# Output matmuls of chosen stretches as four column tiles of TensorE, with a new planner cost for instruction fetch and a new list of departures

## The chip, the cores and the metric

The kernel runs on one core of a Trainium2 chip. The time is the device time of one execution in microseconds (us), as the median of its runs. PE is TensorE, ACT ScalarE, DVE VectorE, POOL GpSimd and SP the engine that issues most DMAs here.

## The reference

An attention over 32 inducing points comes first, then a two-way maxout layer; the output of the first is the input of the second.

```python
def mab(q, kv):                      # scale = 1/sqrt(128)
    s = scale * (q @ kv.transpose(0, 2, 1))
    s = s - s.max(-1, keepdims=True)
    a = np.exp(s)
    a /= a.sum(-1, keepdims=True) + 1e-09
    return a @ kv
h = mab(I, x)                        # I: (4, 32, 128), x: (4, 12544, 128)
y = mab(x, h).reshape(50176, 128)
out = np.maximum(y @ w1, y @ w2) @ w_out     # w1, w2: (128, 1024), w_out: (1024, 128)
```

## The kernel before

The four batches of `x` have 98 chunks of 128 tokens each. Pooling (`mab(I, x)`) of batch 0 is done in the opening, about the first 23 us. Pooling of batches 1 to 3 is interleaved with the second part of the batch before: `pool_scores` (L329, scores of 16 chunks on column tiles), an exponential on ACT, a transpose by DMA (`pool_turn`) and `pool_accum` (L385, the weighted sum, on column tiles). The small matmuls of `small_rep` to `small_m1` then give the pooled `h` of a batch and, from it, `hwd` = h times (w2 - w1) and `m1` = h times (w1 w_out).

The second part works on the identity max(a, b) = a + relu(b - a). With the attention weights e of a chunk (32 inducing points by 128 tokens), a + relu(b - a), times `w_out`, is e times `m1` plus relu(e times `hwd`) times `w_out`. Four quarters of the array's rows work on four chunks side by side:

- `stage` (L610) computes scores of up to 16 chunks on four column tiles, ACT takes the exponential into `e2`.
- `phase` issues one row wave (L1069): four row tiles of 32 rows, each into a PSUM bank of its own. A tile is either a unit of b - a ("U", `hwd` by `e2`, 512 columns in all) or the linear part of a group ("L", `e2` by `m1`). A unit's bank is read by ACT (L1085) or DVE (L1088), which writes relu to SBUF and frees the bank.
- `final_one` issues one output matmul (L876): 128 relu features of one chunk against 128 rows of `w_out`, on the full array, added to the group's bank. Eight of them per chunk, 3136 in all.
- `dens` (L671) sums the attention weights for the denominators; `evict_group` (L907) multiplies by the reciprocal on DVE, and the stores go out from the SP queue.

PE changes its tiling between row waves (`row`), column-tiled jobs (`col`) and everything else (`full`).

The order of all engines' instructions is written out while the program is built. A planner, the class `Clock`, keeps a time for PE, ACT, DVE and the eight PSUM banks; it adds a constant for each step (`PAIR`, 0.0558 us, for an output matmul; `SWITCH` for a change of tiling). The loop at L1248 asks at each step whether a wave's banks are free by that time, whether the next output matmul's relu is ready, and whether a column job is due (`column_work`: a `stage`, a `pool_scores` or a `pool_accum`; jobs fall due by the number of finished chunks), and issues the one or the other. `DEV` is a list of departures: by the step's number it says that a wave is held back (1), put forward (2), that no column job may come (3) or that one may come sooner (4).

```python
            early = 0.2 if ck.mode == "col" else 0.0
            now = tp <= ck.pe + early or tp <= tf and tf > ck.pe
            if how == 1 and tf < INF:
                now = False
            if how == 2 and tp <= ck.pe + 0.2:
                now = True
```

Every program on PE is a stream of pairs, one weight load and one matmul. A column-tiled matmul (`tile_position` (0, 32 p)) uses 32 columns of the array and writes 32 partitions of PSUM; four with different p stand side by side.

Of the kernel before, what the change touches and what calls it, by code (L numbers as in the profile page):

```python
# [19 lines left out]
class Clock:  # L20
# [3 lines left out]
    SWITCH = {"full": 0.11, "row": 0.097, "col": 0.097}  # L24
    LAT = 0.20
    SEM = 0.05

    def __init__(self):
        self.pe = self.act = self.dve = 0.0
        self.mode = "full"  # L30
        self.bank = [0.0] * 8
        self.idle = {}
        self.log = []
        self.busy = {}

# [6 lines left out]
    def run(self, us, mode="full", ready=0.0, why="data"):  # L42
        if mode != self.mode:
            self.pe += self.SWITCH[mode]
            self.busy["sw"] = self.busy.get("sw", 0) + self.SWITCH[mode]
            self.mode = mode
        self.wait(ready, why)
        self.pe += us
        self.busy[mode] = self.busy.get(mode, 0) + us
        return self.pe + self.LAT  # L50

# [51 lines left out]
def kernel(  # L103
# [9 lines left out]
    nc = tc.nc  # L113
# [82 lines left out]

    with tc.manual_schedule(engines={ET.PE, ET.DVE, ET.Activation, ET.Pool, ET.SP}):
# [32 lines left out]
        def p1_transpose(i, piece):  # L230
            k0, n = parts[0][i]
            g, m = COPY[i][piece][:2]
            bi, ps = bank([128, 8, 128], F16)
            for j in range(m):
                nc.tensor.transpose(ps[:, j, :], xn_at[0, i][:, g + j, :], identity16)  # L235
# [17 lines left out]
        def p1_scores(i):  # L253
# [3 lines left out]
            for j in range(n):  # L257
                nc.tensor.matmul(  # L258
                    out=ps[:, j * M : (j + 1) * M],
                    lhsT=xT_tiles[0][:, k0 + j, :],  # L260
                    rhs=inducingT,
                    start=True,
                    stop=True,
                )
# [15 lines left out]
        def p1_esum(i):  # L280
# [4 lines left out]
            for m in pieces(n):  # L285
                nc.tensor.matmul(
# [11 lines left out]
        def p1_hsum(i, lo=0, hi=P1):  # L298
# [3 lines left out]
            for j in range(lo, min(hi, n)):  # L302
                nc.tensor.matmul(  # L303
# [19 lines left out]
        def pool_scores(b, u):  # L323
# [4 lines left out]
            for g in range(4):  # L328
                nc.tensor.matmul(  # L329
# [16 lines left out]
        def pool_rest(b):  # L346
# [3 lines left out]
            for j in range(REST):  # L350
                nc.tensor.matmul(
# [17 lines left out]
        def pool_accum(b, u):  # L369
# [10 lines left out]
            for v in (u - 1, u):  # L380
                eT = st[b]["eT", v][0]
                st[b]["sum", v] = True
                for j in range(4):
                    for g in range(4):
                        nc.tensor.matmul(  # L385
# [8 lines left out]
            if last:  # L394
                et = st[b]["et"][0]
                for g in range(4):
# [6 lines left out]
                    for lhsT, rhs, lo, n in pairs:  # L403
                        nc.tensor.matmul(
# [21 lines left out]
        def small_rep(b):  # L426
# [3 lines left out]
            nc.tensor.matmul(out=ps[:, 0 : C + 1], lhsT=repd, rhs=st[b]["hacc"], start=True, stop=True)  # L430
# [8 lines left out]
        def small_h(b):  # L439
# [3 lines left out]
            nc.tensor.transpose(ps[:, 0:128], st[b]["h4"], identity16)  # L443
# [23 lines left out]
        def small_hwd0(n, eng=0):  # L467
# [8 lines left out]
            nc.tensor.matmul(out=ps, lhsT=st[0]["hT4"], rhs=w21[:, sl], start=True, stop=True)  # L476
# [9 lines left out]
        def small_sums():  # L486
# [3 lines left out]
            nc.tensor.matmul(out=ps[:, 2:3], lhsT=rep32, rhs=es, start=True, stop=True, skip_group_check=True)  # L490
# [7 lines left out]
        def small_hwd(b):  # L498
            st[b]["hwd"] = smp.tile([128, J], F16, name=f"hwd_{b}", tag="hwd")
            hwd = st[b]["hwd"]  # L500
            for half in range(2):
# [3 lines left out]
                nc.tensor.matmul(out=ps, lhsT=st[b]["hT4"], rhs=w21[:, sl], start=True, stop=True)  # L505
# [9 lines left out]
        def small_m1(b):  # L515
            bi, ps = bank([128, 512])
            ck.wait(max(ck.bank[bi], st[b]["hT4r"]), "p1")
            nc.tensor.matmul(out=ps[:, 0:128], lhsT=st[b]["hT4"], rhs=w1out, start=True, stop=True)
# [22 lines left out]
        def weights_2(g, eng):  # L541
            bi, ps = bank([128, 4, 128], F16)
            ck.wait(ck.bank[bi], "w")
            for j in range(4):
                jb = 4 * g + j
                nc.tensor.transpose(ps[:, j, :], w1h[:, 128 * jb : 128 * (jb + 1)], identity16)
# [8 lines left out]
        def weights_3():  # L555
            bi, ps = bank([128, 512])
            ck.wait(max(ck.bank[bi], w_of["w1T"]), "w")
            for jb in range(NJB):
                nc.tensor.matmul(
# [36 lines left out]
        def stage(blk, now=True):  # L596
# [4 lines left out]
            for q in range(4):  # L601
# [7 lines left out]
                for t, c, n in pieces:  # L609
                    nc.tensor.matmul(  # L610
# [45 lines left out]
        def dens(blk):  # L656
# [11 lines left out]
            for blk in blks:  # L668
                wd = blk.width
                for t in range(wd):  # L670
                    nc.tensor.matmul(  # L671
# [8 lines left out]
            end = ck.run(0.029 * n)  # L680
# [30 lines left out]
        def fill(n):  # L711
            bi, ps = bank([128, 512])
            for _ in range(n):
                nc.tensor.matmul(out=ps, lhsT=warm[:, 0:128], rhs=warm, start=True, stop=True)
            ck.run(0.22 * n)
# [5 lines left out]
        for _ in range(WARM):  # L721
            nc.tensor.matmul(out=ps, lhsT=warm[:, 0:128], rhs=warm, start=True, stop=True)
# [29 lines left out]
        def p1_inducing():  # L752
            bi, ps = bank([128, 512])
            nc.tensor.transpose(ps[:, 0:M], ind_sb, identity32[0:M, 0:M])
# [37 lines left out]
        state = {"g": 0, "mm": 0, "lin": 0, "done": 0, "issued": 0}  # L792
# [28 lines left out]
        def keep_busy(until):  # L821
# [6 lines left out]
            turn = ck.SWITCH["full"] if ck.mode != "full" else 0.0  # L828
# [3 lines left out]
            for _ in range(n):  # L832
                nc.tensor.matmul(  # L833
# [5 lines left out]
                    skip_group_check=True,  # L839
                )  # L840
            ck.run(0.11 * n)
# [3 lines left out]
        def linear_last(end):  # L845

            while held:
                g = held[0]
                if g.full:
                    if st[g.blk.b].get("m1r", INF) > ck.pe:  # L850
                        return
                    for s, (q, t) in enumerate(g.chunks):
                        nc.tensor.matmul(  # L853
# [5 lines left out]
                            skip_group_check=True,  # L859
                        )  # L860
                    end = ck.run(0.056 * len(g.chunks))
                evict_group(held.pop(0), end)

        def final_one():
# [4 lines left out]
            if g.ps is None:  # L869
# [6 lines left out]
            nc.tensor.matmul(  # L876
# [5 lines left out]
                skip_group_check=True,  # L882
            )
            end = ck.run(ck.PAIR)
# [75 lines left out]
        def want_linear():  # L960
# [32 lines left out]
        }  # L993
        LIMIT = -16
# [16 lines left out]
        def phase(jobs):  # L1011
# [13 lines left out]
            if ck.mode != "row":  # L1025
                ck.pe += ck.SWITCH["row"]
                ck.mode = "row"
# [38 lines left out]
            for i in range(4):  # L1066
                for seq in parts_:
                    if i < len(seq):
                        nc.tensor.matmul(**seq[i])  # L1069
# [177 lines left out]
        step = -1  # L1247
        while state["g"] < len(groups) or held:  # L1248
            step += 1
            how = DEV.get(step, 0)  # L1250
            side_work()
            if held and ck.mode == "full":
# [14 lines left out]
            early = 0.2 if ck.mode == "col" else 0.0  # L1267
# [52 lines left out]
```

## Time and profile before

| | |
|---|---|
| median of 3 runs | 325.12 us (324.23 to 325.51) |
| span of the profiled execution | 322.5 us (its page gives no time beside the span) |
| PE busy | 315.6 us, 5375 matmuls and as many weight loads |
| ACT busy, DVE busy | 281.8 us, 281.4 us |
| output matmuls (L876) | 3136, 216.9 us |
| row waves (L1069) | 888 matmuls by `hwd`, 381 by `e2` |

The span runs from the first to the last instruction of the profiled execution; the time of a run also holds what lies before and after it. Matmuls are pipelined, so a matmul's duration is longer than its distance to the next one. In the views of groups and of instructions in order of time, "L876" is line 876 of the kernel before, names are out<-in, and the idle time of an engine stands behind a bar or in brackets with what ended it.

### The profile page before, as it was taken

How to read it: one execution, taken by the hardware profiler on the slowest of the kernel's cores; microseconds unless marked ns; L12 is line 12 of the kernel's file. 1: busy time of each engine (PE TensorE's matmuls, PEld its weight loads, DVE VectorE, ACT ScalarE, POOL GpSimd, SP SyncE). 2: the span in 40 equal slices, each digit the busy share in tenths (PEclk: the TensorE clock that was granted, in tenths of full speed). 3: DMA queues.
4: the chain of work that ended last, by engine and by line, in shares of the span. 5: the costliest groups of instructions: out<-in, count | busy, mean ns of one | idle time of the engine just before them, and what ended most of it. 6: DMA issues, size and time to landing. Idle time of an engine off the chain costs nothing.

```text
span 322.5 us, 12605 instructions
## 1 busy us (share of the span) xinstructions
PE 315.6 (98%) x5375; PEld 239.8 (74%) x5375; DVE 281.4 (87%) x508; ACT 281.8 (87%) x561; POOL 37.8 (12%) x90
## 2 busy tenths in 40 slices
PE   7899999999999999999999999999999999999996
PEld 3776777777777777777777777777777777777786
DVE  3369999988989998999989989988998999899974
ACT  3779999998978999999898999998869999999960
POOL 7470000000040000000040000000006400302000
PEclk9999999999999999999999999999999999999999
DMA  8999999954279999794279999893424322324233
GB/s 205 207 268 213 218 249 203 210 136 133 100 150 245 221 254 216 181 194 139 99 151 242 218 258 207 160 211 120 118 96 103 135 80 100 109 100 128 87 118 116
DMA packets 77320, 53.99 MB, mean 167 GB/s; under 512 B 56112, under 2 KB 64976, under 8 KB 77264
## 3 DMA queue, kind: packets, MB, share of 16 engines
q1 hardware_dynamic: 71232, 39.42, 50.0%
q0 software_dynamic: 5888, 13.70, 21.7%
q8 instruction: 42, 0.69, 0.9%
q14 instruction: 14, 0.11, 0.1%
q10 hardware_dynamic: 144, 0.07, 0.1%
HBM read 27.28 MB, written 25.69 MB: 164 GB/s over the span
## 4 chain that ended last, share of the span: by engine, by line
PE 93%; DMA 5%; ACT 1%; issue 1%; POOL 0%; DVE 0%; POOLq 0%
PE ps L876 62%; PE ps L1069 22%; DMA xn<-in_x_dram 5%; PE ps L610 2%; PE ps L385 2%; PE ps L329 1%; PE ps L671 1%; PE ps L833 1%; ACT e L629 0%; PE ps L505 0%; ACT hwd L482 0%; PE ps L235 0%; PE ps L303 0%; PE ps L430 0%; PE ps L258 0%
## 5 line engine op out<-in xcount | busy, mean ns | idle before, releaser
L1085 ACT ACTIVATE relu<-ps 128x512 f16<-128x512 f32 x462 | 244.1, 604 | 23.0 <-PE ps L1069 15.0
L1088 DVE TENSOR_SCALAR relu<-ps 128x512 f16<-128x512 f32 x322 | 206.1, 682 | 16.2 <-PE ps L1069 14.8
L876 PE MATMUL ps<-woutp,relu 128*128 128x128 f16 x3136 | 216.9, 220 | 0.0
L876 PEld LDWEIGHTS <-relu 128*128 128x128 f16 x3136 | 176.6, 98 | 39.4 <-issue 28.9
L1069 PE MATMUL ps<-e,hwd 32*128 32x512 f16 (+2 forms) x888 | 88.2, 358 | 0.1
L907 DVE TENSOR_TENSOR o<-ps,rp 128x512 f32<-128x512 f32 (+3 forms) x80 | 51.2, 640 | 1.8 <-PE ps L876 1.3
L1069 PEld LDWEIGHTS <-hwd 32*128 32x128 f16 x888 | 24.5, 91 | 20.9 <-issue 0.8
L1069 PE MATMUL ps<-m,e 32*128 32x128 f16 x381 | 38.7, 217 | 0.0
L1069 PEld LDWEIGHTS <-e 32*128 32x128 f16 x381 | 21.2, 92 | 2.9 <-issue 0.4
L907 DVE TENSOR_TENSOR o<-ps,rpt 128x512 f32<-128x512 f32 (+3 forms) x28 | 17.3, 618 | 4.1 <-PE ps L853 2.2
L166 POOL DMA_DIRECT2D xn<-in_x_dram x33 | 17.8, 553 | 6.7 <-DMA xn<-in_x_dram 4.6
L164 POOL COPY pace<-hacc 128x1 f32<-128x1 f32 x2 | 0.4, 188 | 133.1 <-DVE hacc L418 133.1
L246 DVE COPY xT<-ps 128x768 f16<-128x768 f16 (+6 forms) x11 | 4.8, 458 | 8.9 <-PE ps L235 8.9
L340 ACT ACTIVATE eu<-ps 128x512 f16<-128x512 f32 x18 | 10.9, 614 | 0.1
L629 ACT ACTIVATE e<-ps 128x512 f16<-128x512 f32 (+2 forms) x21 | 10.4, 568 | 0.2 <-PE ps L610 0.2
L235 PE MATMUL ps<-identity,xn 128*128 128x128 f16 x98 | 8.1, 219 | 2.3 <-DMA xn<-in_x_dram 1.8
L535 POOL COPY m1bd<-m 32x128 f16<-32x128 f16 x4 | 1.1, 287 | 76.7 <-DVE m L530 76.6
L249 ACT COPY xT<-ps 128x768 f16<-128x768 f16 (+5 forms) x10 | 6.5, 671 | 3.0 <-PE ps L235 2.9
L698 POOL TENSOR_TENSOR w1T<-den 128x256 f32<-128x256 f16 (+1 forms) x7 | 4.4, 633 | 38.6 <-DMA den<-e 38.6
L700 POOL TENSOR_TENSOR w1T<-w1T 128x64 f32<-128x64 f32 (+4 forms) x28 | 8.4, 302 | 2.2
L235 PEld LDWEIGHTS <-xn 128*128 128x128 f16 x98 | 5.6, 97 | 4.0 <-DMA xn<-in_x_dram 2.2
L610 PE MATMUL ps<-xT,hT 128*32 128x512 f16 (+3 forms) x114 | 8.2, 361 | 0.0
(93 smaller groups left out, 117.0 us busy)
## 6 DMA issues: line engine op xcount, KB each, us to landing
out_dram<-o SPq DMA_DIRECT2D x68, 256.0 KB, 2.8
xn<-in_x_dram POOLq DMA_DIRECT2D x24, 448.0 KB, 10.1
out_dram<-o SPq DMA_DIRECT2D x54, 128.0 KB, 1.8
wf<-in_moe_w_dram POOLq DMA_DIRECT2D x4, 256.0 KB, 5.9
xn<-in_x_dram POOLq DMA_DIRECT2D x3, 224.0 KB, 8.8
xT<-xn SPq DMA_TRANSPOSE x42, 3.8
xf<-in_x_dram SPq DMA_DIRECT2D x1, 512.0 KB, 3.7
xf<-in_x_dram SPq DMA_DIRECT2D x1, 384.0 KB, 4.2
```

Of the source, the lines that this page charges most:

```text
L166: nc.gpsimd.dma_start(out=xn_at[b, i][lo:hi, 0:n, :], in_=xr[b, lo:hi, k0 : k0 + n, :])
L235: nc.tensor.transpose(ps[:, j, :], xn_at[0, i][:, g + j, :], identity16)
L249: nc.scalar.copy(out=dst, in_=ps[:, 0:m, :])
L340: nc.scalar.activation(out=eu, in_=ps, func=AF.Exp, scale=scale, accum_out=st[b]["es"][:, u : u + 1])
L610: nc.tensor.matmul(out=ps[32 * q : 32 * (q + 1), 128 * t : 128 * (t + n)], lhsT=hq, rhs=xT[:, c : c + n, :], start=True, stop=True, tile_p ...
L629: nc.scalar.activation(out=blk.e2[:, lo:hi], in_=ps[:, lo:hi], func=AF.Exp, scale=st[0]["rs"] if blk.b == 0 else scale,)
L700: nc.gpsimd.tensor_add(acc[:, :, 0:n], acc[:, :, 0:n], acc[:, :, n : 2 * n])
L876: nc.tensor.matmul(out=g.ps[:, 128 * c : 128 * (c + 1)], lhsT=g.blk.relu[q][:, 128 * (jb * w4 + t) : 128 * (jb * w4 + t + 1)], rhs=woutp[: ...
L907: nc.vector.tensor_mul(osb[:, 0:n, :], g.ps[:, 0 : n * C].rearrange("p (s c) -> p s c", s=n), rp)
L1069: nc.tensor.matmul(**seq[i])
L1085: nc.scalar.activation(out=dst, in_=src, func=AF.Relu)
L1088: nc.vector.tensor_scalar(out=dst, in0=src, scalar1=0.0, scalar2=None, op0=ALU.max)
```

## The change

Four things change; what is computed stays.

1. A new helper `as_tiled` issues a matmul as it was when the planner's mode is not `col`, and as four column tiles (the four quarters of the weights' columns, each into its 32 partitions of the same bank) when it is. Output matmuls, denominators, the filler of `keep_busy` and the last linear parts go through it. PE so stays in column tiling after a column job, until the next wave.
2. A new set `COLUMNS` names 32 row waves by number. After such a wave the first output matmul puts the planner's mode to `col`, whether a column job has been there or not.
3. The planner counts PE's instructions (two for each matmul) and has a cost for their fetch: blocks of 256, a queue of 64, 4.0 us each. These are constants of the code. Its cost of a change to column tiling goes from 0.097 to 0.11, and `EARLY` is 0 where it was 0.2.
4. The some 200 departures keyed by step number are replaced by 6, keyed by wave, output matmuls since the wave, and repetition.

```diff
-    SWITCH = {"full": 0.11, "row": 0.097, "col": 0.097}
+    SWITCH = {"full": 0.11, "row": 0.097, "col": 0.11}
+    FIRST, SLOTS, QUEUE, FETCH = 185, 256, 64, 4.0
...
     def run(self, us, mode="full", ready=0.0, why="data"):
         if mode != self.mode:
-            self.pe += self.SWITCH[mode]
...
+            self.enter(mode)
         self.wait(ready, why)
+        n = self.pc - self.pc0
+        while n and self.edge <= self.pc:
+            self.wait(self.landed - us * (self.edge - self.pc0) / n, "fetch")
+            k = len(self.past) - 1
+            while k and self.past[k][0] > self.edge - self.QUEUE:
+                k -= 1
+            self.landed = max(self.past[k][1], self.landed) + self.FETCH
+            self.edge += self.SLOTS
...
+    def matmul(*a, **k):
+        ck.pc += 2
+        nc.tensor.matmul(*a, **k)
...
+    def as_tiled(out, lhsT, rhs, start, stop):
+
+        if ck.mode != "col":
+            matmul(out=out, lhsT=lhsT, rhs=rhs, start=start, stop=stop, skip_group_check=True)
+            return "full"
+        for p in range(4):
+            r = slice(32 * p, 32 * (p + 1))
+            matmul(
+                out=out[r, :],
+                lhsT=lhsT[:, r],
+                rhs=rhs,
+                start=start,
+                stop=stop,
+                tile_position=(0, 32 * p),
+                skip_group_check=True,
+            )
+        return "col"
...
             w4 = g.blk.quarters[q].w
-            nc.tensor.matmul(
+            if ck.mode == "row" and state["phase"] in COLUMNS:
+                ck.enter("col")
+            mode = as_tiled(
                 out=g.ps[:, 128 * c : 128 * (c + 1)],
                 lhsT=g.blk.relu[q][:, 128 * (jb * w4 + t) : 128 * (jb * w4 + t + 1)],
                 rhs=woutp[:, jb, :],
                 start=(g.full and state["mm"] == 0),
                 stop=(jb == NJB - 1 and not g.full),
-                skip_group_check=True,
             )
-            end = ck.run(ck.PAIR)
+            end = ck.run(ck.PAIR, mode)
...
         DEV = {
-            20: 2, 33: 2, 58: 1, 77: 1, 95: 1, 97: 1, 99: 1, 103: 1, 104: 1, 106: 4, 116: 1, 127: 2, 130: 1,
...
+            50800: 2, 61200: 2, 70900: 2, 141400: 1, 201400: 1, 1541600: 1
         }
+        COLUMNS = {
+            29, 34, 37, 43, 56, 64, 72, 73, 79, 85, 89, 91, 93, 116, 121, 128, 137, 141, 146, 153, 155, 156,
+            162, 166, 168, 170, 173, 177, 178, 180, 183, 185
+        }
+        EARLY = 0.0
...
-            if held and ck.mode == "full":
+            if held and ck.mode != "row":
                 linear_last(0.0)
...
-            early = 0.2 if ck.mode == "col" else 0.0
+            early = EARLY if ck.mode == "col" else 0.0
```

`dens`, `keep_busy` and `linear_last` call `as_tiled` in the same way; all other matmuls and transposes go through the counting helpers and are otherwise unchanged.

More of the change, by code (lines that the diff above doesn't have):

```diff
@@ L429, in small_rep @@
             ck.wait(ck.bank[bi], "p1")
-            nc.tensor.matmul(out=ps[:, 0 : C + 1], lhsT=repd, rhs=st[b]["hacc"], start=True, stop=True)
+            matmul(out=ps[:, 0 : C + 1], lhsT=repd, rhs=st[b]["hacc"], start=True, stop=True)
             end = ck.run(0.28)
@@ L475, in small_hwd0 @@
             ck.wait(max(ck.bank[bi], st[0]["hT4r"]), "p1")
-            nc.tensor.matmul(out=ps, lhsT=st[0]["hT4"], rhs=w21[:, sl], start=True, stop=True)
+            matmul(out=ps, lhsT=st[0]["hT4"], rhs=w21[:, sl], start=True, stop=True)
             end = ck.run(0.215 * w / 512)
@@ L489, in small_sums @@
             ck.wait(ready, "p1")
-            nc.tensor.matmul(out=ps[:, 2:3], lhsT=rep32, rhs=es, start=True, stop=True, skip_group_check=True)
+            matmul(out=ps[:, 2:3], lhsT=rep32, rhs=es, start=True, stop=True, skip_group_check=True)
             end = ck.run(0.11)
@@ L517, in small_m1 @@
             ck.wait(max(ck.bank[bi], st[b]["hT4r"]), "p1")
-            nc.tensor.matmul(out=ps[:, 0:128], lhsT=st[b]["hT4"], rhs=w1out, start=True, stop=True)
+            matmul(out=ps[:, 0:128], lhsT=st[b]["hT4"], rhs=w1out, start=True, stop=True)
             end = ck.run(0.06)
@@ L713, in fill @@
             for _ in range(n):
-                nc.tensor.matmul(out=ps, lhsT=warm[:, 0:128], rhs=warm, start=True, stop=True)
+                matmul(out=ps, lhsT=warm[:, 0:128], rhs=warm, start=True, stop=True)
             ck.run(0.22 * n)
@@ L721 @@
         for _ in range(WARM):
-            nc.tensor.matmul(out=ps, lhsT=warm[:, 0:128], rhs=warm, start=True, stop=True)
+            matmul(out=ps, lhsT=warm[:, 0:128], rhs=warm, start=True, stop=True)
         for n in ("h", "e"):
@@ L827, in keep_busy @@
                 return
-            turn = ck.SWITCH["full"] if ck.mode != "full" else 0.0
+            turn = ck.SWITCH["full"] if ck.mode == "row" else 0.0
             n = int((until - ck.pe - turn - 0.1) / 0.11)
```

75 lines of the change are left out of this document (44 added, 31 removed), and 16 rows, old and new, of the table DEV.

## The prediction

> **What bounds the kernel now.** I read the page first, then PE's waits, then the instructions in order of time around a column-tiled job. In the page the reader is to see that PE is busy for nearly the whole span and carries the chain that ended last, that its clock is not throttled, and that its instructions come through a DMA queue of their own, q8.
>
> ```profile
> PE 315.6 (98%) x5375; PEld 239.8 (74%) x5375; DVE 281.4 (87%) x508; ACT 281.8 (87%) x561; POOL 37.8 (12%) x90
> ...
> PEclk9999999999999999999999999999999999999999
> DMA  8999999954279999794279999893424322324233
> ...
> q8 instruction: 42, 0.69, 0.9%
> ...
> PE 93%; DMA 5%; ACT 1%; issue 1%; POOL 0%; DVE 0%; POOLq 0%
> PE ps L876 62%; PE ps L1069 22%; DMA xn<-in_x_dram 5%; PE ps L610 2%; PE ps L385 2%; PE ps L329 1%; PE ps L671 1%; PE ps L833 1%; ACT e L629 0%; PE ps L505 0%; ACT hwd L482 0%; PE ps L235 0%; PE ps L303 0%; PE ps L430 0%; PE ps L258 0%
> ```
>
> PE's share of 98% does not say whether it works or only changes its tiling, so the waits come next: who PE waited for (us in all, times, longest). All four rows belong to the opening (lines 235, 722 and 476 are the first batch's transposes, the warm-up and the first weights), 3.6 us together. In the steady part PE waits for nobody for a time that the view counts. The two rows of the reluing engines say the reverse: they wait for PE's waves.
>
> ```profile
> PE ps L235 <- DMA xn<-in_x_dram: 1.8, 3, 1.0
> PE ps L722 <- DVE warm L216: 1.2, 1, 1.2
> PE ps L235 <- ACT xn L719: 0.4, 1, 0.4
> PE ps L476 <- DVE w L779: 0.2, 1, 0.2
> ...
> ACT relu L1085 <- PE ps L1069: 15.0, 34, 1.6
> DVE relu L1088 <- PE ps L1069: 14.8, 41, 1.2
> ```
>
> So the time is the sum of PE's issue steps, and the view to cost an edit from is PE's instructions in order of time (start, time, what, count). A matmul's own duration is latency; the next one's start is its cost.
>
> ```profile
> 56.37 0.40 PE L1069 MATMUL ps<-e,hwd 32*128 32x512 f16 x4
> 56.70 0.40 PE L610 MATMUL ps<-xT,hT 128*32 128x512 f16 x4
> 56.92 0.62 PE L329 MATMUL ps<-xT,inducingT 128*32 128x512 f16 x8
> 57.48 0.73 PE L876 MATMUL ps<-woutp,relu 128*128 128x128 f16 x10
> ...
> 75.92 0.39 PE L1069 MATMUL ps<-e,hwd 32*128 32x512 f16 x2
> 75.93 0.22 PE L1069 MATMUL ps<-m,e 32*128 32x128 f16 x1
> 75.93 0.38 PE L1069 MATMUL ps<-e,hwd 32*128 32x512 f16 x1
> 76.00 0.33 PE L1069 MATMUL ps<-m,e 32*128 32x128 f16 x3
> 76.25 0.95 PE L876 MATMUL ps<-woutp,relu 128*128 128x128 f16 x14
> 77.14 0.40 PE L1069 MATMUL ps<-e,hwd 32*128 32x512 f16 x4
> 77.47 1.08 PE L385 MATMUL ps<-xn,eT 128*32 128x128 f16 x64
> 78.48 0.51 PE L876 MATMUL ps<-woutp,relu 128*128 128x128 f16 x6
> 78.92 0.39 PE L1069 MATMUL ps<-e,hwd 32*128 32x512 f16 x4
> 79.24 0.90 PE L876 MATMUL ps<-woutp,relu 128*128 128x128 f16 x13
> ...
> 103.23 0.45 PE L876 MATMUL ps<-woutp,relu 128*128 128x128 f16 x5
> 103.52 0.34 PE L671 MATMUL ps<-ones_q,e 128*128 128x4 f16 x8
> 103.72 0.77 PE L876 MATMUL ps<-woutp,relu 128*128 128x128 f16 x11
> ```
>
> One row of the groups, apart by shape, gives the latency (behind the bar: busy us, mean ns of one, idle before):
>
> ```profile
> L876 PE MATMUL ps<-woutp,relu 128*128 128x128 f16 x3136 | 216.9, 220 | 0.0
> ```
>
> Four prices come out of it. An output matmul (L876): 14 of them take 0.95 us with the last one's latency, 0.220, so (0.95 - 0.22) / 13 = 0.056 us each. A set of four tiles with 512 columns (a wave L1069, or L610): 56.70 to 56.92, 0.22. A denominator matmul (L671): 103.52 to 103.72 for 8, 0.025 each. And a change of tiling: from 75.92 to 79.24 lie 3.32 us with three waves (0.66), 14 + 6 output matmuls (1.12) and 16 column sets of L385 (0.90); 0.64 us are left for six changes (row to full, full to row, row to column, column to full, full to row, row to full), **0.107 us each**. The three kinds do not differ by more than the rows' rounding.
>
> **The change part by part.**
>
> *Fewer changes of tiling.* Counted in the order of PE's instructions: both programs have 223 row waves. Between two waves, before, 196 times only full-array work stands, 19 times column then full, 5 times full, column, full and 3 times full then column: 196 x 2 + 19 x 3 + 5 x 4 + 3 x 3 = 478 changes. After, it is full 177 times, column alone 42 times, full then column 3 times, and once full, column, full: 451. So 27 changes go, 27 x 0.107 = **2.9 us** off PE, which is the path. Of the 42 column stretches 14 hold nothing but output matmuls; there row, column, row takes the place of row, full, row and nothing is saved. The gain is from the stretches that hold a column job.
>
> *576 of 3136 output matmuls become four column tiles each* (the order has 2304 tiles). The nearest row is L385, the same shape as such a tile: 64 in 1.08 us, sixteen sets of four, (1.08 - 0.22) / 15 = 0.057 us a set against 0.056 for the full matmul.
>
> ```profile
> L385 PE MATMUL ps<-xn,eT 128*32 128x128 f16 x288 | 5.5, 220 | 0.0
> ```
>
> I take no cost, because the 0.057 includes the slower first step after a change, which is priced above; the upper end is 576 x 0.001 = 0.6 us. What covers it: the four tiles stream side by side. Without that cover a set would cost up to four steps. The Trainium skill, page TensorE: Matmul & The Clock Gate, Part 1, "Wait — 56ns, not 53.3ns?", has a rule against this change: matmuls never start closer together than about 25 ns however small, which would make a set 100 ns. By that rule the sum would be 25 us worse. The trace disagrees: the 288 matmuls of L385 are 5.5 us, 19 ns each with latencies, and the sixteen sets of 75.9 to 79.2 us held 57 ns through their 128 instructions.
>
> *32 of the 76 denominator matmuls become four tiles as well* (in the order: 44 full, 128 tiles). No row shows column tiles with 4 columns. Lower end 0.025 a set, as L671, nothing lost; upper end 0.057, as L385, 32 x 0.032 = 1.0 us. I take the middle, **+0.5 us**, since either row is equally near: the one has the small moving size, the other the tiling.
>
> *More instructions.* 14387 rows on PE after, 10739 before. q8 moved 42 packets, so 256 instructions each; after, 57. At 0.9% of sixteen engines' 322.5 us a packet takes 46 / 42 = 1.1 us. I take nothing for 15 more, since they run beside PE; the risk is below.
>
> *A new order.* The old list of some 200 departures, which steered single steps, gives way to 6 and to the planner's changed costs. PE's waits show nothing in the steady part that a new order could win, so the lower end is 0; it could lose if a wave stands where its PSUM banks are not yet free. Behind a late wave everything on PE is queued, and ACT and DVE wait for it. The stores and transposes on the SP queue keep their number (173 rows both), and move with the groups that they belong to. I take 0, with an upper end of 1 us.
>
> *Sum:* -2.9 + 0 + 0.5 + 0 + 0 = **-2.4 us**: a span of 320.1 instead of 322.5. The profiled execution gives only its span; the median of the timed runs is 325.12, 2.6 more, for what lies around the span. I carry that over: 325.12 - 2.4 = **322.7 us**. With all upper ends (0.6 + 1.0 + 1.0) it is 324.8; with none of the costs 322.2.
>
> **The rivals.**
>
> *The saved changes turn into waits for relu (324.3).* ACT and DVE are at 87% over the span, and about 92% in the densest stage:
>
> ```profile
> 100.00:200.00 100.00, 100.00 (x1687) 75.53 (x1684) 92.79 (x162) 92.77 (x187) 3.89 (x8) 1.00 0.92 198
> ```
>
> (columns: stretch, its length, then PE, PEld, DVE, ACT and POOL busy with counts, clock, DMA.) If their order fits badly, a wave waits for its banks: two thirds of the net 2.4 us given back are 1.6, so 324.3. Against it: a kernel faster by 1% needs 93.7 of 100 us from them, still under PE, and they had 15.0 and 14.8 us of waiting for PE's waves.
>
> *PE's instructions come too late (327.7, slower).* A normal gap between waves has 8 instructions of the wave and 28 of 14 output matmuls in some 1.2 us. A column gap of 13 sets has 8 + 104 = 112 in the same time: 0.22 + 13 x 0.056 + 2 x 0.107 = 1.16 us. A block of 256 holds two column gaps and one normal one, 3.5 us instead of 7 to 8. 45 stretches with column outputs make some 20 such blocks, and I guess half of them that dense. If a fetch takes over 3.5 us from request to landing, the rest is idle PE: at 0.5 us for ten blocks 5.0, 322.7 + 5.0 = 327.7. It decides from 0.24 us a block, where the 2.4 are gone. For it: the DMA engines are 90% busy in several slices, so a request can queue. Against it: 1.1 us a packet, and "issue" only 1% of the chain. The Trainium skill, page Runtime: NRT & Kernel Launch, "Instruction fetch mechanics", says that blocks of 256 are fetched while the current one runs and that crossing one is mostly hidden; by that this rival costs nothing. The trace agrees on the 256, and no run here shows a block used up in 3.5 us.
>
> *A set costs four steps of 0.025 (about 348).* L671's 0.025 us from one small matmul to the next may be a floor of any matmul; a set would then cost 4 x 0.025 = 0.100, and 576 x (0.100 - 0.056) = 25 us come on top. L385's rows speak against it; a longer stretch than its sixteen sets (the longest has 21) could still run into it.
>
> **How the numbers follow.** Within 0.5%, 1.6 us, a measurement of this kernel can hardly tell from no change: faster is below 323.5, slower above 326.7. The forecast, 0.63: PE is the path, and all its terms are in rows. Waits for relu, 0.23. Late instructions, 0.11. Four steps a set, 0.02; 0.01 for an order that costs more than any of these. So faster 0.63, same 0.23, slower 0.14. The range: below, 322.2 less 0.5 for the run to run spread (the lowest run before is 0.9 under its median), 321.7; above, the waits for relu with all upper ends of the forecast's terms, 324.8 + 0.9 = 325.7, the 0.9 being that same spread. The slower cases, 0.14, lie outside.
>
> **What would show it.** Right: 451 changes of about 0.107 us, output matmuls as sets of four tiles with 0.056 to 0.057 us from set to set, PE still without waits after the opening, a span near 320. Denominator sets at 0.025 or 0.057 decide the 0.5. Wrong: gaps on PE at fixed distances of 256 instructions with nothing released before them (late instructions); sets that slow down after the first eight or sixteen (the step floor); rows of PE waiting for ACT or DVE at the waves (relu).

## The result and the profile after

The changed kernel takes 328.61 us (327.15 to 330.77, 4 runs) beside 325.31 us (324.23 to 325.93, 4 runs) for the kernel before on the same chip: ratio 1.0111, 95% interval 1.0073 to 1.0149. It is slower by 1.1%; the forecast was 322.7. In the table of the experiments, two of the ten runs of neworder_needed (331.97 and 335.78 us) fell in a slower state of the chip and are left out of its row, while every other row has all its runs.

The page of the kernel after, the lines that answer to those shown of before:

```profile
PE 315.4 (97%) x7199; PEld 241.7 (74%) x7199; DVE 280.2 (86%) x505; ACT 283.5 (87%) x564; POOL 38.2 (12%) x90
...
PEclk9999999999999999999999999999999999999999
DMA  7999999994259999997479999996315533223233
...
q8 instruction: 56, 0.92, 1.2%
...
PE 87%; DMA 5%; ACT 2%; SPq 2%; DVE 2%; POOL 1%; issue 1%; POOLq 0%; ACTq 0%
```

PE is busy for as long as before (315.4 against 315.6 us) in a span 2.9 us longer, 325.4 against 322.5, and its share of the chain that ended last fell from 93% to 87%. What took its place are small shares of ACT, DVE, SP's queue and POOL: PE now waits for others.

PE's waits after, with the line numbers of the new file (L216 is the helper through which nearly all matmuls go, L220 that of the transposes; who is waited for, then us in all, times, longest):

```profile
PE ps L220 <- DMA xn<-in_x_dram: 2.3, 3, 1.0
PE ps L216 <- DVE warm L259: 1.2, 1, 1.2
PE ps L216 <- issue: 1.2, 2, 1.0
PE ps L216 <- ACT eu L383: 0.7, 1, 0.7
...
PE ps L216 <- DMA xT<-xn: 0.3, 1, 0.3
```

The first two belong to the opening. The other three are new, and all lie in the steady part. "issue" means that the profile shows nothing that PE waited for. The instructions of PE in order of time show where the longest such wait stands:

```profile
59.47 0.80 PE L216 MATMUL ps<-woutp,relu 128*32 128x128 f16 x44
60.10 0.39 PE L216 MATMUL ps<-xT,inducingT 128*32 128x512 f16 x4
60.31 0.27 PE L216 MATMUL ps<-ones_q,e 128*32 128x4 f16 x17
61.54 0.26 PE L216 MATMUL ps<-ones_q,e 128*32 128x4 f16 x15 [0.95 <-issue]
61.63 0.57 PE L216 MATMUL ps<-woutp,relu 128*32 128x128 f16 x28
```

A run of 32 denominator tiles stops in the middle of a set of four, after the seventeenth, for about a microsecond. The view names no data that was late. Counted over PE's weight loads and matmuls, the stop lies at an edge between two blocks of 256 instructions.

The wait for ACT is another matter. All engines from 69.9 us on:

```profile
69.96 2.54 SPq L409 DMA_TRANSPOSE eT<-eu  x2
...
70.00 0.39 PE L216 MATMUL ps<-e,hwd 32*128 32x512 f16 x2
70.36 0.60 ACT L383 ACTIVATE eu<-ps 128x512 f16<-128x512 f32 x1 [1.33 <-DMA eT<-eu]
...
71.10 0.39 PE L216 MATMUL ps<-e,hwd 32*128 32x512 f16 x2 [0.72 <-ACT eu L383]
```

ACT has the next pooling exponential (`eu`) to write, but its buffer is one of five, and the DMA transpose that reads the old contents has not landed. ACT stands for 1.33 us, the PSUM bank that the `eu` would have freed stays taken, and the row wave stands in its middle for 0.72 us behind it.

**Where the time went.** I summed PE's matmuls from start to start from the first wave on, and split off as pauses what a step took beyond its usual length, where that was about 0.1 us or more. Before: 296.3 us, of it 0.9 in pauses, so 295.4 of steps. After: 298.2, of it 4.1 in pauses, so 294.1 of steps. The steps got 1.3 us shorter, and the pauses 3.2 us longer. The other 0.9 of the span's 2.9 us is the opening: the first wave starts at 24.04 instead of 23.13 us. That is no part of the change: the opening is the same work in both kernels, and in the profiles of this case with that opening the first wave starts anywhere from 22.9 to 25.0 us. The granted clock is no part of it either: from 25 to 320 us it was 1.00 in both profiles.

### The profile page after: what moved, and what is told of

Its sections match the earlier page's. It is cut to its first block, busy times and chain, and to the rows that moved or that the text cites. A ratio compares the mean times of both kernels' runs of the same rounds, so it can differ in the third digit from the quotient of the medians.

```text
span 325.4 us, 16261 instructions
## 1 busy us (share of the span) xinstructions
PE 315.4 (97%) x7199; PEld 241.7 (74%) x7199; DVE 280.2 (86%) x505; ACT 283.5 (87%) x564; POOL 38.2 (12%) x90
## 4 chain that ended last, share of the span: by engine, by line
PE 87%; DMA 5%; ACT 2%; SPq 2%; DVE 2%; POOL 1%; issue 1%; POOLq 0%; ACTq 0%
PE ps L216 86%; DMA xn<-in_x_dram 3%; DMA xT<-xn 1%; SPq L189 1%; DVE relu L1121 1%; POOL xn L183 1%; ACT relu L1118 1%; PE ps L220 1%; DVE o L950 0%; SPq L978 0%; ACT e L672 0%; ACT hwd L525 0%; POOL identity masks.py:199 0%; POOL identity masks.py:197 0%; ACT eu L383 0%
## 5 line engine op out<-in xcount | busy, mean ns | idle before, releaser
L216 PE MATMUL ps<-woutp,relu 128*128 128x128 f16 (+1 forms) x4864 | 220.8, 220 | 0.2 <-issue 0.2
L216 PEld LDWEIGHTS <-relu 128*128 128x128 f16 (+1 forms) x4864 | 180.2, 97 | 39.2 <-issue 26.3
L216 PE MATMUL ps<-e,hwd 32*128 32x512 f16 (+2 forms) x888 | 88.8, 358 | 0.7 <-ACT eu L383 0.7
L216 PEld LDWEIGHTS <-hwd 32*128 32x128 f16 x888 | 24.8, 91 | 22.2 <-issue 2.3
L216 PE MATMUL ps<-m,e 32*128 32x128 f16 x381 | 38.8, 217 | 0.0
L216 PEld LDWEIGHTS <-e 32*128 32x128 f16 (+2 forms) x564 | 25.8, 93 | 4.5 <-issue 1.3
L220 PE MATMUL ps<-identity,xn 128*128 128x128 f16 x98 | 8.1, 219 | 3.0 <-DMA xn<-in_x_dram 2.3
L220 PEld LDWEIGHTS <-xn 128*128 128x128 f16 x98 | 5.6, 97 | 4.6 <-DMA xn<-in_x_dram 2.6
L216 PE MATMUL ps<-xT,hT 128*32 128x512 f16 (+3 forms) x114 | 8.9, 360 | 0.0
L216 PE MATMUL ps<-xT,inducingT 128*32 128x512 f16 x72 | 7.1, 379 | 0.3 <-DMA xT<-xn 0.3
```

The costliest lines, as they stand in the source:

```text
L216: nc.tensor.matmul(*a, **k)
L220: nc.tensor.transpose(*a, **k)
```

## The experiments

Two theories for the pauses, and one for the small gain:

- **Fetch.** The next block of 256 PE instructions arrives some 4 us after the one before it. A stretch full of column sets uses a block up faster than that, and PE stands at the edge.
- **Order.** The new list of departures leaves less time between a transpose and its reader; with PE's steps shorter, some transposes come late.
- **Pace.** Even without any pause, PE time that is removed comes back in part as waits of the waves for relu.

All results in one table. The ratio is to the kernel before on the same chip, with its 95% interval. The last three columns are of the profiled execution, from the first wave on: PE's steps without pauses, pauses at block edges, and pauses for late data of 0.15 us and more (pauses of neither kind are left out).

| kernel | median us | ratio | steps | edges | late data |
|---|---|---|---|---|---|
| before | 325.2 | 1 | 295.4 | 0 | 0 |
| after | 328.61 | 1.0111 [1.0073, 1.0149] | 294.1 | 1.9 | 1.3 |
| after_again | 330.51 | 1.0154 [1.0135, 1.0173] | 294.3 | 3.3 | 2.2 |
| neworder_full | 328.79 | 1.0106 [1.0067, 1.0144] | 299.0 | 0 | 0 |
| after_two | 330.46 | 1.0171 [1.0131, 1.0210] | 300.1 | 0 | 0 |
| neworder_needed | 326.7 | 1.0050 [1.0023, 1.0077] | 294.1 | 1.3 | 1.6 |
| neworder_after | 329.63 | 1.0155 [1.0110, 1.0200] | 297.6 | 0.4 | 2.6 |
| after_shift | 331.02 | 1.0191 [1.0145, 1.0238] | 294.4 | 3.9 | 0.2 |
| after_eu | 327.05 | 1.0075 [1.0048, 1.0103] | 294.2 | 3.8 | 1.6 |
| needed_eu | 326.9 | 1.0071 [1.0035, 1.0106] | 294.4 | 1.1 | 0.2 |
| replanned | 332.31 | 1.0210 [1.0186, 1.0234] | 296.1 | 3.6 | 2.0 |
| oldorder_tiles | 324.95 | 0.9991 [0.9969, 1.0013] | 294.5 | 0 | 0 |
| oldorder_drop | 324.21 | 0.9968 [0.9954, 0.9982] | 294.6 | 0 | 0 |
| oldorder_alltiles | 489.65 | 1.5047 [1.4899, 1.5196] | | | |

The changed kernel itself was run again (after_again) on another chip and came out 1.9 us above its first median, with pauses at the same places, two more at edges (at 45 and 147 us) and one more for a late transpose (at 120 us). So rows of different calls differ by that much for no reason in the code; the profiled run of after_eu (330.45 us) was the slowest of its eight.

> The changed kernel once more beside the two others on the same chip, for its spread: 328.6 as at first, 1.011 times before. Its profile shows the pauses at the block edges of 60, 180, 186 and 227 us again (late instructions: same places, other lengths, as the fetch's time changes), and the wait for eT at 70 us.

**The tiles' parts, new order.** In `as_tiled`, the set of four may be issued as one full matmul instead, while the planner goes on as if it were a set:

```diff
+        if whole():
+            matmul(out=out, lhsT=lhsT, rhs=rhs, start=start, stop=stop, skip_group_check=True)
+            ck.pc += 6
+            return "col"
```

`neworder_full` has `whole()` always true: the new order with no output tiles, 509 changes of tiling.

> The changed kernel's order on every engine, but each set of four column tiles is one full-array matmul again. PE has 10751 instructions as before (14399 in the changed kernel) and 509 changes of tiling (478 before, 451 changed). Theory 'late instructions': the 1.9 us of pauses at block edges in the changed kernel's trace go; against before only 31 more changes at 0.107 us stand, 3.3 us, so about 328.6. Theory 'the new order costs': the waits at 70 us (ACT for eT, 0.9) and at 129 us (scores for xT, 0.4) stay in the trace, and the time is above 328.6 by what the order costs, 1.5 to 3 us more: 330 to 332.

PE has neither of the new kinds of wait; its rows are those of the opening alone:

```profile
PE ps L216 <- DVE warm L266: 1.2, 1, 1.2
PE ps L220 <- DMA xn<-in_x_dram: 0.7, 1, 0.7
PE ps L220 <- DVE inducingT L805: 0.6, 1, 0.6
PE ps L216 <- DVE w L829: 0.2, 1, 0.2
```

It is as slow as the changed kernel, but for another reason: its 31 changes more than before cost 3.0 us (48.4 against 45.4 us in the steps at which the tiling changes, 0.097 each). So the edges' pauses need the tiles, and PE waits for no late data where its steps are 4.9 us longer; ACT still waits 0.4 us for the transpose of `eu`, which does not reach PE.

`neworder_needed` leaves tiles only in the stretches that hold a column job (`state["phase"] in` the 14 others gives a full matmul): 378 sets, the same 451 changes.

> The changed kernel's order, with sets of tiles only in the stretches that hold a column job; the 14 listed stretches without one have full matmuls (378 sets instead of 576). Changes of tiling stay at 451, PE has 13211 instructions instead of 14399. Late instructions: fewer dense blocks, so most of the 1.9 us of pauses at block edges goes: 1 to 2 us under the changed kernel, about 327. The new order costs: no change from the changed kernel, 328.6 less 0.3 for the cheaper matmuls.

It has the steps of the changed kernel, 294.1 us, with a third fewer sets, and still pauses for 1.1 us at 60.7 (an edge) and for 1.25 us at 70.3 (the `eT` transpose). The sets in the 14 stretches gain nothing, as predicted. Its pauses at edges, 1.3 us, are below the 1.9 and 3.3 us of the two profiles of the changed kernel.

`neworder_after` has tiles only behind a column job, 336 sets (304 of output matmuls, 32 of denominators).

> The changed order with sets only behind the column job of a stretch, full matmuls ahead of it and in stretches without one: 469 changes of tiling, 336 sets, 12767 instructions on PE. It is to the new order what the old order with tiles (324.95) is to the old. Late instructions are the whole loss: no dense blocks, 9 fewer changes than before, so 324.5 to 325.5. The new order costs by itself: the wait for eT at 70 us stays, and the time is 326 to 327.

It came out above both expectations. Only 0.4 us of pauses are left at edges, and yet it is 1.5% slower; ACT waits 2.3 us for the transpose of `eu`, PE 1.5 us for ACT:

```profile
ACT eu L393 <- DMA eT<-eu: 2.3, 1, 2.3
...
PE ps L216 <- ACT eu L393: 1.5, 1, 1.5
...
PE ps L216 <- issue: 0.2, 1, 0.2
```

So pauses for late data alone, 2.6 us here, can be as long as those at the edges of the changed kernel. Here 3.5 us more of steps come on top (469 changes and dearer output steps), so the run does not price the order by itself.

**Moving the edges.** `after_shift` adds 64 matmuls of one column to the warm-up. That is 128 instructions, half a block. Five of the nine wide warm-up matmuls become one-column ones too; everything behind the warm-up is as it was:

```diff
-        for _ in range(WARM):
+        for _ in range(WARM - 5):
...
+        for _ in range(5 + 64):
+            nc.tensor.matmul(out=ps[:, 0:1], lhsT=warm[:, 0:128], rhs=warm[:, 0:1], start=True, stop=True)
```

> The changed kernel with 64 more one-column matmuls (128 instructions, about 1.6 us at 0.025 each) in the warm-up, where 5 of 9 wide ones become one-column ones too. The rest of the order is the same, but every block edge of 256 instructions comes 64 matmuls earlier in the work. Late instructions: the pauses of the changed kernel at 60, 180, 186 and 227 us, which stand at instruction 185 + 256 k, vanish; new ones stand where the moved edges meet dense stretches, near 62, 120 and 217 us, 1 to 3 us together; the time is within 1.5 us of the changed kernel. If the pauses belong to the work (a wait, a bank), they stay at 60, 180, 186 and 227.

The pauses of the changed kernel at 60, 180, 186 and 227 us are gone; others of 0.6 to 1.1 us stand at 63, 100, 123 and 222 us, half a block on, and a short one at 232. They are 3.9 us together where 1 to 3 were expected, and the time is 2.4 us above the first median of the changed kernel and 0.5 above the second, with hardly a pause for late data left: pauses at edges alone can go with the whole loss. PE in order of time in after_shift, where the changed kernel had stopped among the denominators:

```profile
61.30 0.46 PE L216 MATMUL ps<-ones_q,e 128*32 128x4 f16 x32
61.60 0.76 PE L216 MATMUL ps<-woutp,relu 128*32 128x128 f16 x40
62.28 0.39 PE L216 MATMUL ps<-e,hwd 32*128 32x512 f16 x4
62.61 0.45 PE L216 MATMUL ps<-woutp,relu 128*128 128x128 f16 x5
64.04 0.62 PE L216 MATMUL ps<-woutp,relu 128*128 128x128 f16 x8 [0.98 <-issue]
```

The 32 denominator tiles now run through, and PE stops 64 pairs later (the 15 denominator tiles that had been left, 40 + 4 + 5 matmuls), among plain output matmuls that before never stopped. The pause belongs to the count of instructions and not to any instruction or its data. This shows the fetch. The packets of q8 agree: in the profiles of these kernels, the packet with the block at whose edge PE stopped for 0.2 us or more had landed 1.2 to 1.6 us before PE went on. In the kernel before, every block of the steady part had landed at least 2.3 us before its first use.

**What a fetch costs.** `oldorder_alltiles` is the kernel before with every output matmul and denominator as four tiles, so that nearly all blocks are dense:

```diff
-            nc.tensor.matmul(
+            tiled[0] = True
+            as_tiled(
```

> The order of before with every output matmul and denominator as four column tiles: 30026 instructions on PE, 492 changes of tiling. It measures the fetch by itself. Without a limit: 14 x 0.107 + 3136 x 0.0014 + 76 x 0.012 = 6.8 us more than before, 332. Late instructions: 117 blocks of 256, each used up in about 2.5 us, so the time is 117 times what one fetch takes from request to use: 350 us at 3 us each, 410 at 3.5, 470 at 4.

Its page and PE's waits:

```profile
PE 358.1 (73%) x15011; PEld 259.0 (53%) x15011; DVE 290.5 (59%) x508; ACT 287.4 (58%) x561; POOL 37.8 (8%) x90
...
q8 instruction: 117, 1.92, 1.7%
```

```profile
PE ps L206 <- issue: 115.8, 96, 3.5
```

PE stands for 115.8 us in 96 pauses. All 96 lie at edges. 491.5 us for 117 packets are 4.2 us a block (the opening included; the median from packet to packet is 3.8), while each packet takes 1.1 us of the queue's busy time (1.7% of sixteen engines, 491.5 us). In between, the sets of this stretch run at full pace:

```profile
201.58 1.02 PE L206 MATMUL ps<-woutp,relu 128*32 128x128 f16 x60
202.54 0.39 PE L1088 MATMUL ps<-e,hwd 32*128 32x512 f16 x4
202.86 0.79 PE L206 MATMUL ps<-woutp,relu 128*32 128x128 f16 x42
204.64 0.34 PE L206 MATMUL ps<-woutp,relu 128*32 128x128 f16 x10 [0.99 <-issue]
```

Sixty tiles and the change behind them take 0.96 us, about 57 ns a set. Over the whole run a set took 62 ns, at a mean granted clock of 0.957. The rival of four steps of 25 ns a set is refuted, on stretches as long as any of the changed kernel.

**Fewer instructions for the same tiling.** `after_two` takes two tiles of 64 columns instead of four of 32:

```diff
-        for p in range(4):
-            r = slice(32 * p, 32 * (p + 1))
+        for p in range(2):
+            r = slice(64 * p, 64 * (p + 1))
...
-                tile_position=(0, 32 * p),
+                tile_position=(0, 64 * p),
```

> The changed kernel with each set as two column tiles of 64 instead of four of 32: the same order, 11967 instructions on PE instead of 14399. Column jobs keep 32 columns, so sets of 64 next to them may or may not be a change of tiling. If a change of width costs nothing: 451 changes and no dense blocks, the changed kernel without its pauses at block edges, 2 to 3 us less, 326. If a change of width costs 0.107 like any other: 509 changes, 58 x 0.107 = 6.2 us more and no pauses, as the same order without tiles, 328.8.

No pause at an edge is left, nor any for late data, but the changes are back at 509: going from tiles of 32 columns to tiles of 64 costs what any change costs. In order of time, two sets with 512 columns, then tiles of 64:

```profile
58.43 0.60 PE L216 MATMUL ps<-xT,inducingT 128*32 128x512 f16 x8
58.96 0.92 PE L216 MATMUL ps<-woutp,relu 128*64 128x128 f16 x26
```

From 58.43 to 58.96 are 0.53 us for two sets of 0.22 and the change, so 0.09. The time is 1.7 us above the 328.8 expected for this case: PE's steps are 1.1 us longer than in neworder_full, and the first wave of the profiled run starts 1.3 us later (24.23 against 22.97 us). The Trainium skill, page TensorEngine Tiling (Array Packing), "Key Properties", says that a change of the tiling mode drains TensorE while a change of tile within one does not. The trace agrees, by the 0.09 us that this change cost, with the width of a tile as part of the mode.

**The late transpose.** `after_eu` has a sixth buffer for `eu` (`bufs=6` for 5 in both places).

> The changed kernel with six buffers instead of five for the exponentials of pooling, so that the sixth unit of a batch need not wait until the first one's transpose has been read; the same order on every engine and the same block edges. The new order costs: ACT's wait of 1.3 us for eT at 70 us and PE's wait of 0.9 us behind it go, and the time falls by 0.9 us or a little more, to about 327.6. Late instructions alone: the time stays at 328.6 and the pauses at block edges stay.

The wait of ACT for `eT<-eu` is gone, and the median is 1.6 us under the changed kernel's in the first comparison, with intervals that overlap; against after_again they do not. In the profiled run a wait of 1.6 us for the transpose of `xT` stands at 148 us, so not every late transpose comes from the buffer. `needed_eu` joins this to neworder_needed, with one more stretch (wave 29, the edge near 60 us) as full matmuls.

> The changed order with tiles only in stretches that hold a column job, not in the stretch at 60 us either (453 changes of tiling, 357 sets, PE 13037 instructions), and six buffers for pooling's exponentials. From 327.6 (the same without the last two): the pause of 1.1 us at 60 us and the wait of 1.25 us at 70 us go, two changes of tiling come back (0.2): 325.4, as before. If the waits only move to the next place, 327 or more.

This is a miss by 1.5 us. Its profiled run, the fastest of five (325.35), still has 1.1 us at edges, now at 187 and 219 us. The median is no better than that of either part alone.

**A plan with more margin.** `replanned` is the changed kernel with the planner's fetch cost at 5.0 us, transposes planned later, and departures and stretches chosen again by the planner's own clock:

```diff
-    FIRST, SLOTS, QUEUE, FETCH = 185, 256, 64, 4.0
+    FIRST, SLOTS, QUEUE, FETCH = 185, 256, 40, 5.0
...
-                return d.get(("T", (U * a[1] + U - 1) // (P1 // 2)), INF) + 8.0 <= now
+                return d.get(("T", (U * a[1] + U - 1) // (P1 // 2)), INF) + 9.0 <= now
```

> The changed kernel planned again with the measured margins: 5.0 us for a fetch (4.0 in the changed kernel) and 40 instructions ahead (64), 9 us for a transposed x (8), 1 us more for a transposed exponential, and a pooling unit that reuses a buffer only 3 us after its transpose was issued; another list of 14 departures and 22 stretches. 452 changes of tiling, 470 sets, 13580 instructions on PE. If the pauses at block edges and the waits for late transposes were the loss: both are gone from the trace, and 26 x 0.107 = 2.8 us less, 470 x 0.0014 = 0.7 us more and some of it given back in the waves as in the old order with tiles, so 323.5 to 324.5. If only the fetch was: 325 to 326, with waits for transposes left. If a cause is missing: 327 or more.

A miss by 8 us. PE in order of time around two of its three pauses at edges:

```profile
186.47 0.27 PE L216 MATMUL ps<-m,e 32*128 32x128 f16 x2
187.70 0.23 PE L216 MATMUL ps<-m,e 32*128 32x128 f16 x1 [0.91 <-issue]
...
192.84 0.79 PE L216 MATMUL ps<-woutp,relu 128*128 128x128 f16 x11
195.00 0.34 PE L216 MATMUL ps<-woutp,relu 128*128 128x128 f16 x3 [1.37 <-issue]
```

The block from 187.70 on lasted some 6 us and was not dense: mostly full matmuls, with one column stretch. The fetch was slow: the packet of the block used at 195.00 started at 192.54, 4.8 us after the edge at 187.70, so edge to use is 7.3 us. Loads of the next batch's x, six issued by POOL from 170.4 us on, were on the DMA engines, with the transposes behind them. That these held up the packet is the likely reading; no run removes them. The windows (stretch, length, engines' busy time, clock, DMA share, GB/s) of that stage and of the rest of the steady part:

```profile
174.00:196.00 22.00, 18.65 (x445) 13.88 (x446) 16.97 (x30) 17.41 (x35) 0.00 (x0) 1.00 1.11 227
196.00:300.00 104.00, 104.00 (x2364) 80.23 (x2360) 95.12 (x167) 95.89 (x193) 13.91 (x39) 1.00 0.59 134
```

In this stage, at a DMA share of 1.11, the time from edge to use was not 4 us but up to 7, and the transpose of `eu` was late by 2.7 us in an earlier busy stage of the same run. The changed kernel has this too: in after_again the pause at 189 us ended a block of 6.8 us, in a stage with a DMA share of 1.10 (176 to 190 us). So no single constant for a fetch describes it.

The third pause, 1.1 us at 180.4, stands in a wave:

```profile
181.50 0.09 PEld L216 LDWEIGHTS <-hwd 32*128 32x128 f16 x1 [1.27 <-issue]
181.51 0.38 PE L216 MATMUL ps<-e,hwd 32*128 32x512 f16 x1 [0.97 <-ACT relu L1118]
```

The matmul's row names a relu, but that relu had ended at 181.16. The weight load ahead of the matmul waits for nothing and came only at 181.50, at a block's edge and 1.3 us after its packet had landed, so the table counts this pause to the edges; without the late block, the relu would still have kept PE for some 0.8 us of it.

**The gain itself.** `oldorder_tiles` keeps the old list, and only leaves the output matmuls behind a column job in column tiling until the next wave: 224 sets, 458 changes instead of 478.

```diff
+            tiled[0] = ck.mode == "col" or tiled[0] and ck.mode == "full"
-            nc.tensor.matmul(
+            as_tiled(
```

> The order of before on every engine with its 200 departures; only the output matmuls between a column job and the next wave become four column tiles (224 sets). 458 changes of tiling instead of 478, PE 12098 instructions. Both theories: 20 x 0.107 = 2.1 us less, 224 x 0.0014 = 0.3 us more for the sets, so 323.5, without pauses at block edges and without waits for late transposes. If tiles cost something of their own that neither theory has: 325 or more.

No pause comes, and the time does not move: ratio 0.9991, with 1 in the interval. The steps at changes fell by 1.9 us (45.4 to 43.5), and 1.0 us of them came back in the steps of the waves (52.0 to 53.0). `oldorder_drop` is the kernel before without the two output matmuls behind each column job:

```diff
+            if ck.mode == "col":
+                drop[0] = 2
+            if drop[0] > 0 and 0 < jb < NJB - 1:
+                drop[0] -= 1
+            else:
```

> The kernel before, with 46 output matmuls left out, two after each column job (46 x 0.056 = 2.6 us of PE's work, about as much as the saved changes of tiling, without tiles and without more instructions); the output lacks their terms. If PE's steps are all that bounds: 2.6 us less, 322.6. If ACT and DVE keep their pace and PE waits for banks in many small pieces (the waits for relu): about half of it comes back, 1 to 1.5 us less, 324. The old order with tiles had 1.9 us less of changes in its trace, and 1.0 us more in its row waves.

2.6 us of PE's work are gone (46 matmuls of 0.056), and the median falls by 0.9 us, with the waves 1.5 us longer. ACT's and DVE's waits for PE's waves are nearly those of before, 28.1 us in all against 29.8, as the waits of oldorder_drop have them:

```profile
ACT relu L1091 <- PE ps L1075: 14.7, 33, 1.7
DVE relu L1094 <- PE ps L1075: 13.4, 38, 1.1
```

So PE's time that is removed here is worth about a third of itself (0.9 of 2.6 us). The rest stands in the start-to-start times of the waves, in pieces too small for PE's waits, which have no row for them.

No version that does the whole work beat the kernel before by more than a measurement can tell.

## Why the prediction was wrong

The forecast was 2.4 us faster; the median is 3.3 us slower.

- **Fewer changes, −2.9: the count right, the term too large.** Changes fell from 45.4 to 42.8 us, 2.6 us for 27, 0.096 each.
- **Sets at no cost, upper end 0.6: it was just above the upper end.** 576 sets took 33.3 us, 57.9 ns each against 56.5 ns for a full matmul; all output matmuls together went from 177.3 to 178.0 us, 0.7.
- **Denominators +0.5: right.** 1.95 became 2.42 us; a column set took 0.035 to 0.039 us, between the two ends taken.
- With the waves' 0.45 us more and jobs' 0.35 less, the steps gave 1.3 us where −2.4 stood (−2.6 + 0.7 + 0.5 + 0.1 by these rows). The rival of saved changes turned into relu waits was about this: on the old order it is what oldorder_tiles and oldorder_drop show. In the changed kernel it is a small part.
- **"More instructions: I take nothing" is the step that failed first.** I argued from 1.1 us a packet, which is the time that a packet keeps the DMA engines busy, and not the time from one block to the next where PE has to wait for each, 4.2 us by oldorder_alltiles. The blocks of before last 7.8 us in the median and 5.9 at least, so its trace did not show a fetch that comes late; "they run beside PE" held for those blocks only. The rival of late instructions had this mechanism and its condition (a fetch over 3.5 us), and was given 0.11. Its price was put at ten blocks of 0.5 us, 5.0 us; measured were four to six pauses of 0.15 to 1.2 us, 1.9 and 3.3 us in the two profiles of the changed kernel. The rule of the Trainium skill set beside it, page Runtime: NRT & Kernel Launch, "Instruction fetch mechanics", that crossing a block is mostly hidden, holds for the kernel before and not here: in oldorder_alltiles 115.8 of 491.5 us are such crossings. The packets were 56, not 57, and the rows of PE 14398 and 10750 by the two pages, which changes nothing in this term.
- **"A new order: I take 0, with an upper end of 1 us" is the step that failed second.** The waits for the transposes of `eu` and `xn` took 1.3 and 2.2 us of PE in the two profiles of the changed kernel. I had looked at what a wave waits for at its banks, and passed over the reuse of `eu`'s five buffers; the SP transposes "keep their number", but what counted was the time between one and the exponential behind it.
- **Four steps a set (348): refuted**, as the prediction had it.
- **What lies around the span** was put at 2.6 us. It is 1.8 (the profiled run after: 327.15 for a span of 325.4); the rest of the 2.6 was that the profiled execution of before had the early opening. This shifts nothing between the two kernels, only the level.
- **The upper end of the range** was said to hold the relu waits and all upper ends. These add up to 324.3 + 2.1 = 326.4; 325.7 holds the upper ends and the spread alone. The measured 328.6 is above both.

The signs asked for were there: gaps at fixed distances of 256 instructions with nothing released before them, and a row of PE waiting for ACT at a wave.

**Open:** how the median's 3.3 us divide between fetch and transposes in the runs that have no profile. The two profiles have 1.9 + 1.3 and 3.3 + 2.2 us, and taking part of one away (after_eu, neworder_needed) gave 1.6 to 1.9 us against the first comparison, with overlapping intervals. needed_eu takes part of both away and is still 1.7 us slower than before. Nor did the runs show why the same kernel's pauses are longer on one chip than on another.

## What to carry to other kernels

Count instructions beside time when an edit multiplies them: PE here could stop at a block's edge when it used up 256 instructions in less than about 4 us (not always: a block of 3.1 us in the changed kernel ran through), however idle the fetch queue looked by its busy share, and in busy DMA stages (a share of 1.1 and more) also when it took over 6. A view of waits with no row for an engine does not make its time free to take: remove a known piece of work and see how much of it comes back before a gain is summed from that engine's steps. And where an order is tuned, look at the slack of each buffer's reuse behind a DMA, since a faster stream reaches the next write sooner.

## What the runs showed of the hardware that I had not expected

- Where PE stops at nearly every edge, a block of 256 instructions takes about 4 us (117 blocks in 491.5 us, 3.8 us in the median from packet to packet), though its packet keeps the queue busy for 1.1 us; in a stage with a DMA share of 1.11 one took 7.3 us.
- A change between column tiles of 32 and of 64 columns costs about 0.09 us, like a change between rows, columns and the full array.
- A column set of four tiles with 4 columns takes 0.035 to 0.039 us, less than one with 128 columns and more than a full matmul's 0.026.
